# Between two halves of a gated attention and FFN kernel: one quarter's parts by way of HBM, a sum made from parts, copies and splits in another order

## The chip, the cores and the metric

One core of one Trainium2 chip. The metric is the device time of one execution in microseconds (us), the median of several runs. Five engines work side by side on their own instruction queues: TensorE (PE) for matmuls, VectorE (DVE), ScalarE (ACT), GpSimd (POOL) and SyncE (SP, which issues most of the DMAs). Each queue is worked off in order, so an instruction that waits holds up everything behind it on its engine.

## The reference

For x of 2048 tokens by 512 columns (all float32):

```python
x = A_x
g = sigmoid((x * gate_w).sum(-1, keepdims=True))
q, k, v = heads(x @ wqkv)                  # 32 heads of 16
a = attention(q, k, v) @ wo                # token s sees s, s-2, ..., s-14
b = (gelu(x @ w_gate) * (x @ w_up)) @ w_down   # 512 -> 1792 -> 512
out = g * a + (1 - g) * b
```

Attention has a window of 8 keys at a distance of 2, so even and odd tokens never meet. The kernel calls the two sets parity 0 and parity 1.

## The kernel before, in words

**Numbers in parts.** For each operand of a matmul the kernel keeps two float32r parts: `hi` is a copy by ScalarE (L770, recorded as L746), and `lo` is the raw value minus `hi`, by VectorE (L773). A product is three matmuls: hi hi, lo hi, hi lo. A weight in parts takes twice its raw size.

**Products by Strassen's scheme.** The large products are cut in quarters a11 to a22 (tokens) and b11 to b22 (weights) and take seven block products instead of eight: a11 b11, a12 b21, s1 t1, s2 t2, s3 t3, s4 b22 and a22 t4, where s1 to s4 and t1 to t4 are sums of quarters (t3 = b22 - b12, t2 = t3 + b11, t4 = b21 - t2). One block (`block`, L788) is 4 row tiles of 6 matmuls, 128 rows by 512 columns. Its result lies in four PSUM banks: `acc0` to `acc3`, or four of tag `p`.

**Stages.** `start` (L825) makes keys and queries of parity 0, and it is there that all sums of the weight quarters are made for the first time; it stores t1 and t2 to HBM (`TS`). Then comes `ffn(0)`, the FFN of the even tokens in 14 steps f, each with gate and up products (L430) and the down product (L473). Then `kq_second` (L1077), in this text **the turn**: keys and queries of parity 1 in seven blocks. Then `ffn(1)`, `out_first` and `finish` (L679), which multiply the attention's results by wo.

**Getting ready for the turn.** `before` (L545) and `ready` (L1040) are generators. During the last steps of `ffn(0)` they are advanced one step at a time, and their steps load raw weights (`load_raw`, L810, 512 KB each into a tile of tag `S`), load the stored t2 (`load_pairs`) and split operands. b11 is loaded raw in `before` and split in `ready`, b12, b21 and b22 are loaded at the head of `ready`, s1 is made at its end.

**The turn itself.** U are the four `acc` banks, V_ and Z_ four banks of tag `p`. a11 b11 goes into U. `out_of` (L798) copies U into V_, so that U can go on with s2 t2 and a12 b21 can be added in V_. Then `put` evicts V_ as keys and queries of tokens, U goes through s2 t2, s3 t3 and a22 t4 with copies `u2` and `u3` between them, and the last two blocks, s1 t1 and s4 b22, are joined with the copies on VectorE (`join`, L801).

**What sets the order.** Splits, copies and sums in the turn go through three `Row` objects, `act`, `row` and `mms` (L734 to 748): each ties an instruction to the one before it on its engine, so ScalarE, VectorE and TensorE keep the order of the program there. All else is placed by a scheduler, which leaves each engine one fixed queue.

**Attention** is a generator too. `pull(budget)` (L336) adds to a credit and advances it until the credit is spent; each `block` of the turn calls it four times with `ASK`. Its work is put far back in priority (`BEHIND`) and is tied to the latest matmul (`paced`), so it fills VectorE: scores (L210, L213), softmax, and the weighted sum of the values (`mix`: L258, L262, L264, L266, then a transpose, L271, and a store to HBM by SP, L273). The results return as `raw<-os` (L657) and are split by L87 and L88 for `finish`.

**Values.** `values(par, jj)` (L172) makes v of one tile of tokens with matmuls of 258 or 256 columns (L130); those of parity 1 belong to the head of `ffn(1)`.

Of the kernel before, what the change touches and what calls it, by code (L numbers as in the profile page):

```python
# [10 lines left out]
F32 = mybir.dt.float32  # L11
# [5 lines left out]
P = 128  # L17
# [9 lines left out]
WA = 576  # L27
# [4 lines left out]
NU = D // UC  # L32
WARM = 16
FILLERS = 2
ASK = 1.0
BEHIND = 150
PACE = (0.9, 1.0, 1.12)
LOAD = 4.0
# [10 lines left out]
def tile_gated_mix(ctx: ExitStack, tc: tile.TileContext, xt, wqkv, wff, wo, out):  # L49
# [11 lines left out]
    def tl(tag, dt=F32):  # L61
        return pool.tile([P, COLS.get(tag, 512)], dt, name=tag, bufs=BUFS[tag])
# [58 lines left out]
    g = pool.tile([P, 2, NP], F32, name="g")  # L121
    stages = iter(["hh", "hl"] * 99)

    def qkv_mm(ps, par, jj, cb, kcs, c0=0, cn=512):
        t = slice((jj % BT) * P, (jj % BT + 1) * P)
        for kc in kcs:
            xh, xl = X[par, jj // BT, kc]
            wh, wl = WC[cb, kc]
            for n, (a, w) in enumerate(((xh, wh), (xl, wh), (xh, wl))):
                LAST[:] = [nc.tensor.matmul(ps[:, :cn], a[:, t], w[:, c0:c0 + cn], start=(kc == 0 and n == 0),  # L130
                                            stop=(kc == KC - 1 and n == 2))]

    KQ = {}

# [37 lines left out]
    def values(par, jj):  # L172
        for hh in range(2):
            ps = bank(f"acc{(2 * jj + hh) % BT}")
            qkv_mm(ps, par, jj, 1, range(KC), (CU, 0)[hh], (WQ, CU)[hh])
            take(ps, par, jj, hh, tag=None if jj < 5 else "c")
        pull(2.7)
        if jj == NP - 1:
            done.add((par, 1))
# [282 lines left out]
    def down(par, gr, t, b):  # L462
        if b == t == gr == 0:
            ACC.update((t, bank(f"acc{t}")) for t in range(BT))
        pp = bank("p") if b else ACC[t]
        if b and gr:
            nc.scalar.activation(pp, RT[BT + t], AF.Copy)  # L467
        ts = slice(t * P, (t + 1) * P)
        for i in range(2):
            hh_, hl_ = Hs[2 * gr + i, b]  # L470
            d = WD[2 * gr + i]
            for n, (a, w) in enumerate(((hh_, d[:, :512]), (hh_, d[:, 512:1024]), (hl_, d[:, :512]))):
                ins = nc.tensor.matmul(pp, a[:, ts], w, start=(i == 0 and n == 0 and gr == 0),  # L473
                                       stop=(i == 1 and n == 2), skip_group_check=True)
                if gr and b == t == 0 and not par:
                    ordered(ins, LAST[-1])
                LAST[:] = [ins]
        jj = BT * b + t
        if gr == NG - 1 and par:
            nc.scalar.activation(pp, pp, AF.Copy, scale=gc[:, par, jj:jj + 1])  # L480
            ACC[jj] = pp
        elif gr == NG - 1:
            st = tl("scsscscs"[jj])[:, :512]
            nc.scalar.activation(st, pp, AF.Copy, scale=gc[:, par, jj:jj + 1])
            nc.gpsimd.dma_start(out_v[2 * jj], st)
        elif b:
# [58 lines left out]
    def before():  # L545

        room_x(1)
        for k in range(2):
            for i, (n, blk, kc) in enumerate((("a11", 0, 0), ("a12", 0, 2))):
                OP_[n, k], SRC[n, k] = X[1, blk, kc + k], XR[k][:, i * 512:(i + 1) * 512]  # L550
        load_raw("b11", slots("g1", 4), 0, 0)
        yield
        for step in ((), ("a11", 0), (), ("a12", 0)):
            if step:
                hi(*step)
                lo(*step)
            yield

    def ffn(par):
        XOP.update(((n, kc), X[par, blk, kc + k]) for n, blk, k in (("a11", 0, 0), ("a12", 0, 2), ("a22", 1, 2))  # L560
# [195 lines left out]
    def slots(tag, n, w=512):  # L756
        t = tl(tag, F32R)
        return [t[:, i * w:i * w + 512] for i in range(n)]
# [47 lines left out]
        queue.dma_start(rows(QS[par, 1], jj), two[:, 1])  # L806

    TS = {n: dram.tile([4, P, 512], F32, name=f"w{n}") for n in ("t1", "t2")}

    def load_raw(n, rooms_, hh, half):  # L810
        raw = RAWS[n] = tl("S")
# [13 lines left out]
    def start():  # L825
# [26 lines left out]
        load_w(b12, 1, 0)  # L852
        load_w(b22, 1, 1)

        g1a = slots("g1", 4)
# [79 lines left out]
        put(2, V_[2])  # L935
        put(3, V_[3])
        shift(0, nc.sync, 0, BT - 1)
        for k in range(2):
            store("t1", 2 * k, d_[k], 2)
        Z_ = [bank("p") for _ in range(BT)]  # L940
# [96 lines left out]
                XOP[n, kc] = X[0, blk, kc + k]  # L1037
        done.update(((0, 0), (0, 2)))

    def ready():  # L1040

        q = Q2["q"] = [[XR[k][:, i * 512:(i + 1) * 512] for i in range(4)] for k in range(2)]
        load_raw("b12", None, 1, 0)
        load_raw("b21", slots("g0", 3, WA) + slots("c", 1), 0, 1)
        load_raw("b22", None, 1, 1)

        def load_pairs(n):
            t = [tl("d", F32R) for _ in range(2)]
            for k in range(2):
                OP_[n, k] = t[k][:, :512], t[k][:, 512:1024]  # L1050
                load(n, 2 * k, t[k], 2)

        load_pairs("t2")
        yield
# [10 lines left out]
        for k in range(2):  # L1065
            X[1, 1, k] = tl("rt", F32R), tl("rt", F32R)
        name("a21", [X[1, 1, k] for k in range(2)], [q[k][2] for k in range(2)])
# [3 lines left out]
        yield  # L1071
        both(hi, "s1")
        both(lo, "s1")
        yield
        Q2["t1"] = load_pairs

    def kq_second():  # L1077
        for _ in Q2["turn"]:
            pass
        q, s12 = Q2["q"], Q2["s12"]  # L1080
        t4 = slots("g1", 4)
        U = [bank(f"acc{t}") for t in range(BT)]
        block(U, "a11", "b11", True, ask=ASK)
        V_ = [bank("p") for _ in range(BT)]
        for t in range(BT):
            out_of(V_[t], U[t])
        name("t4", pairs(t4), halves(RAWS["b21"]))
        name("b22", pairs(slots("g1", 4)), halves(RAWS["b22"]))
        Q2["t1"]("t1")
        block(V_, "a12", "b21", False, ask=ASK)  # L1090

        def put(jj, ps):
            take_first(1, ps, jj, lambda o, i: act.activation(o, i, AF.Copy))

        for k in range(2):
            sub(s12[k], s12[k], q[k][0])
        both(hi, "s2")
        both(lo, "s2")
        sub(RAWS["b12"], RAWS["b22"], RAWS["b12"])
        name("t3", pairs([x for tag in "sssc" for x in slots(tag, 1)]), halves(RAWS["b12"]))  # L1100
        for t in range(BT):
            put(t, V_[t])
        shift(1, nc.sync, 0, BT - 1)
        both(hi, "t3")
        both(lo, "t3")
        block(U, "s2", "t2", False, ask=ASK)
        sub(RAWS["b21"], RAWS["b21"], RAWS["b11"])
        sub(RAWS["b21"], RAWS["b21"], RAWS["b12"])
        for k in range(2):
            sub(q[k][0], q[k][0], q[k][2])  # L1110
        u2 = [tl("hl")[:, :512] for _ in range(BT)]
        u3 = [tl("hh")[:, :512] for _ in range(BT)]
        both(hi, "s3")
        both(lo, "s3")
        for t in range(BT):
            out_of(u2[t], U[t])
        block(U, "s3", "t3", False, ask=ASK)
        both(hi, "a22", "t4")
        both(lo, "a22", "t4")
        for t in range(BT):  # L1120
            out_of(u3[t], U[t])
        wide = tl("g0")
        for kc in range(KC):
            SRC["v", kc] = raw = (wide[:, kc * WA:] if kc < 3 else tl("c"))[:, :WQ + CU]
            nc.sync.dma_start(raw[:, :CU], wqkv[1, 2, :, kc * WQ:kc * WQ + CU])
            nc.sync.dma_start(raw[:, CU:CU + WQ], wqkv[0, 2, :, kc * WQ:(kc + 1) * WQ])
            t = tl("d", F32R)
            WC[1, kc] = OP_["v", kc] = t[:, :WQ + CU], t[:, VL:VL + WQ + CU]
        block(U, "a22", "t4", False, ask=ASK)
# [4 lines left out]
        both(hi, "a21", "b22")  # L1134
        both(lo, "a21", "b22")
        for k in range(2):
            sub(q[k][1], q[k][1], s12[k])
        both(hi, "s4")
        both(lo, "s4")
        fetch_d(0)  # L1140
        for f in range(2):
            fetch_sums(f)
        for kc in range(2):
            hi("v", kc)
            lo("v", kc)
# [71 lines left out]
```

## Time and profile before

| | us |
|---|---|
| median of 3 runs | 623.4 (622.85 to 623.93) |
| profiled execution, its own time | 622.54 |
| span of the profiled execution | 620.8 |
| PE busy | 600.1 (97%) |
| DVE busy | 532.3 (86%) |
| ACT busy | 390.4 (63%) |
| the turn on PE, first block to last | 287.2 to 344.6 |

The page cuts the span in 40 slices of 15.5 us and gives the busy share of each in tenths, and for PE also the clock that it was granted. Three short stretches stand out, all between 262 and 340 us, where PE stands and the clock falls for a while after it has stood. DVE is nearly as full as PE, ACT has room. DMA moved 132.6 MB.

In the lists, `p<-d,hh` means that a tile of the name p is written from tiles d and hh; `[3.50 <-ACT p L467]` says that the engine stood 3.50 us ahead of the instruction, and that an ACT instruction of line 467, writing p, let it go on. "x24" counts like instructions in a row, and their length is from the first's start to the last's end. Line L746 is the line of `Row`, which stands for every split, copy, sum and matmul that goes through it.

### The profile page before, as it was taken

The page shows a single profiled execution, that of the slowest core. Times are in us where ns is not written, and L with a number is a line of the kernel's source. Part 1 is how long each engine was busy: PE and PEld are TensorE (multiplying, and loading weights), DVE is VectorE, ACT ScalarE, POOL GpSimd, SP SyncE. Part 2 cuts the span into 40 slices and gives each one's busy share as a digit, 9 for nine tenths or more (in the row PEclk, how much of TensorE's full clock was granted, in tenths as well). Part 3 has the DMA queues.
Part 4 walks back from the last instruction along what each step waited for, and adds up shares of the span by engine and source line. Part 5 has one row for each costly group of instructions (what it writes and reads, how often), then busy time and mean ns, then how long its engine had stood idle before and what let it go on. Part 6 is the DMA issues. An engine that isn't in the chain of part 4 may idle for free.

```text
span 620.8 us, 8182 instructions
## 1 busy us (share of the span) xinstructions
PE 600.1 (97%) x2778; PEld 497.8 (80%) x2778; DVE 532.3 (86%) x618; ACT 390.4 (63%) x670; POOL 89.3 (14%) x121
## 2 busy tenths in 40 slices
PE   8999999999999999979697999999999999999997
PEld 6889977788887878858586998888888888888886
DVE  5997979999889898878979789999978898999821
ACT  5844557876887676856454345575757676784541
POOL 0501001111112121102003400110101110201300
PEclk9999999999999999989987999999999999999999
DMA  7689796988899898786616987787797786677723
GB/s 275 217 255 260 224 293 157 283 245 233 217 271 240 220 285 238 188 310 237 194 53 166 279 271 230 174 240 202 200 250 167 217 203 155 192 193 204 122 48 136
DMA packets 80305, 132.60 MB, mean 214 GB/s; under 512 B 8076, under 2 KB 46346, under 8 KB 80264
## 3 DMA queue, kind: packets, MB, share of 16 engines
q1 hardware_dynamic: 62588, 95.84, 47.8%
q0 software_dynamic: 12576, 32.97, 27.0%
q10 hardware_dynamic: 5100, 3.27, 1.7%
q8 instruction: 22, 0.36, 0.2%
q14 instruction: 19, 0.16, 0.1%
HBM read 67.77 MB, written 37.81 MB: 170 GB/s over the span
## 4 chain that ended last, share of the span: by engine, by line
PE 74%; DVE 9%; DMA 8%; issue 4%; ACT 3%; SPq 1%; ACTq 1%; POOL 0%; DVEq 0%; POOLq 0%
PE p L430 33%; PE p L473 11%; PE acc L473 10%; PE p L679 5%; PE acc L746 5%; PE p L746 4%; PE acc L130 4%; DVE prod L258 2%; PE acc L679 2%; DMA d<-r 2%; DVE prod L210 1%; DMA S<-wqkv 1%; DMA kq<-qs 1%; DMA prod<-wqkv 1%; DMA ws<-g 1%
## 5 line engine op out<-in xcount | busy, mean ns | idle before, releaser
L430 PE MATMUL p<-S,g 128*128 128x512 f32 x672 | 166.5, 390 | 0.0
L430 PEld LDWEIGHTS p<-S,g 128*128 128x128 f32 x672 | 125.4, 188 | 26.6 <-ACT rt L489 0.5
L430 PE MATMUL p<-A,g 128*128 128x512 f32 x504 | 127.5, 390 | 0.0
L430 PEld LDWEIGHTS p<-A,g 128*128 128x128 f32 x504 | 94.2, 188 | 19.9 <-DVE c L440 0.3
L210 DVE TENSOR_TENSOR prod<-kq 128x2048 f32<-128x2048 f32 x32 | 73.1, 2284 | 16.2 <-DMA kq<-qs 6.9
L388 POOL DMA_DIRECT2D g<-raw x40 | 34.6, 866 | 284.2 <-ACT g L387 201.8
L258 DVE TENSOR_TENSOR prod<-v,lg 128x2048 f32<-128x2048 f32 x32 | 72.8, 2275 | 3.0 <-PE acc L746 2.5
L213 DVE TENSOR_REDUCE lg<-prod 128x128 f32<-128x2048 f32 x32 | 73.0, 2281 | 0.3
L473 PE MATMUL p<-d,hh 128*128 128x512 f32 x224 | 69.2, 396 | 4.0 <-ACT p L467 3.5
L473 PE MATMUL acc<-d,hh 128*128 128x512 f32 x224 | 61.4, 391 | 1.5 <-DMA d<-r 1.0
L473 PEld LDWEIGHTS p<-d,hh 128*128 128x128 f32 x224 | 42.2, 190 | 14.7 <-ACT p L467 4.9
L473 PEld LDWEIGHTS acc<-d,hh 128*128 128x128 f32 x224 | 41.8, 188 | 11.7 <-DMA d<-r 1.8
L387 ACT ACTIVATE g<-raw 128x1024 fp32r<-128x1024 f32 (+1 forms) x40 | 39.4, 985 | 15.1 <-PE p L746 6.2
L392 ACT ACTIVATE g<-raw 128x1024 fp32r<-128x1024 f32 (+1 forms) x40 | 39.5, 990 | 12.4 <-PE p L430 12.4
L440 DVE TENSOR_TENSOR c<-p,s 128x512 f32<-128x512 f32 x56 | 37.9, 679 | 8.1 <-PE p L430 8.0
L130 PE MATMUL acc<-d,A 128*128 128x258 f32 (+1 forms) x288 | 40.9, 293 | 4.0 <-ACT d L746 2.9
L444 DVE TENSOR_TENSOR c<-c 128x512 f32<-128x512 f32 x56 | 38.2, 682 | 7.6 <-ACT c L541 7.3
L446 ACT ACTIVATE hh<-c 128x512 fp32r<-128x512 f32 x56 | 35.0, 625 | 14.9 <-DVE c L444 14.3
L473 PE MATMUL p<-d,hl 128*128 128x512 f32 x112 | 43.0, 396 | 0.0
L130 PEld LDWEIGHTS acc<-d,A 128*128 128x128 f32 x288 | 38.7, 201 | 5.4 <-ACT d L746 3.3
L435 ACT ACTIVATE s<-p 128x512 f32<-128x512 f32 x56 | 33.0, 592 | 15.8 <-PE p L430 13.9
L447 DVE TENSOR_TENSOR hl<-c,hh 128x512 fp32r<-128x512 f32 x56 | 38.2, 683 | 2.9 <-ACT hh L446 2.7
(181 smaller groups left out, 923.7 us busy)
## 6 DMA issues: line engine op xcount, KB each, us to landing
g<-raw POOLq DMA_DIRECT2D x27, 512.0 KB, 6.9
raw<-wff SPq DMA_DIRECT2D x42, 256.0 KB, 3.4
ws<-g SPq DMA_DIRECT2D x14, 768.0 KB, 5.9
g<-ws SPq DMA_DIRECT2D x14, 768.0 KB, 5.9
r<-wff SPq DMA_DIRECT2D x28, 256.0 KB, 3.9
d<-r POOLq DMA_DIRECT2D x24, 256.0 KB, 6.9
g<-raw POOLq DMA_DIRECT2D x13, 384.0 KB, 6.8
v<-vs SPq DMA_DIRECT2D x8, 512.0 KB, 6.0
```

The source lines that it names most:

```text
L130: LAST[:] = [nc.tensor.matmul(ps[:, :cn], a[:, t], w[:, c0:c0 + cn], start=(kc == 0 and n == 0), stop=(kc == KC - 1 and n == 2))]
L210: paced(nc.vector.tensor_tensor(prod, spans(k, jj), q[:, jj:jj + 2, None, :].to_broadcast([P, 2, W, UC]), op=OP.mult))
L213: nc.vector.tensor_reduce(two_of(lg, jj), prod.rearrange("p j w (h d) -> p (j w) h d", d=DH), axis=AX.X, op=OP.add)
L258: paced(nc.vector.tensor_tensor(prod.rearrange("p j w (h d) -> p (j w) h d", d=DH), spans(v, jj).rearrange("p j w (h d) -> p j w h d", d=D ...
L387: nc.scalar.activation(lo, raw, AF.Copy, scale=-1.0)
L392: ins = nc.scalar.activation(hi, raw, AF.Copy)
L430: LAST[:] = [nc.tensor.matmul(ps, w_, a_, start=(start and kc == 0 and n == 0), stop=(kc == 1 and n == 2), skip_group_check=True)]
L444: nc.vector.tensor_tensor(ge, ge, up, op=OP.mult)
L447: nc.vector.tensor_tensor(hl_, ge, hh_.bitcast(F32), op=OP.subtract)
L473: ins = nc.tensor.matmul(pp, a[:, ts], w, start=(i == 0 and n == 0 and gr == 0), stop=(i == 1 and n == 2), skip_group_check=True)
L679: ins = nc.tensor.matmul(pa, a, b, start=(first and n == 0), stop=(last and n == 2), skip_group_check=True)
L746: return lambda *args, **kw: self.add(getattr(self.eng, name)(*args, **kw))
```

## The change

- b11's two parts are no longer made a second time. `start` stores the tile with both (1 MB, one DMA by SP) in a new HBM tile `TB`, and `before` loads it back in one DMA in place of the raw b11; its splits on ScalarE and VectorE are gone.
- t4 is made as raw b21 minus the two parts of t2 (four subtractions of 128x512) in place of b21 minus b11 minus t3 (two of 128x1024).
- The raw loads of b12, b21 and b22 and the splits of a11 and a12 move ahead, from `ready` into `before`; the splits of s2, and the difference and splits of t3, move ahead from the turn to the end of `ready`. Since `act` keeps the program's order, they now stand ahead of the copies of the first block (U into V_). t3 uses the slots of b21's neighbours in tag g0 and c.
- From then on the copies of a finished block stand ahead of the splits of later ones; the splits of s3, a22, t4, b22, s4 and a21 each move about one block earlier, and the loads of the v weights too.
- The last products of ffn(0) are evicted to other tiles (rt in place of s and c for half of them), so X[1, 1] takes its tiles later.
- `values` of parity 1 for the first two tiles are ordered behind the last matmul that went through `mms`, that is behind s4 b22.
- `ASK`, the attention credit for each row tile of a block, goes from 1.0 to 0.7.

```diff
-ASK = 1.0
+ASK = 0.7
...
+                if behind:
+                    ordered(LAST[-1], behind)
...
-            qkv_mm(ps, par, jj, 1, range(KC), (CU, 0)[hh], (WQ, CU)[hh])
+            qkv_mm(ps, par, jj, 1, range(KC), (CU, 0)[hh], (WQ, CU)[hh], mms.last if par and jj < 2 else None)
...
-            st = tl("scsscscs"[jj])[:, :512]
+            st = tl("rt" if b else "sc"[t % 2])[:, :512]
...
     def before():
...
-        load_raw("b11", slots("g1", 4), 0, 0)
+        t = tl("g1", F32R)
+        nc.sync.dma_start(t.bitcast(F32), TB)
+        name("b11", pairs([t[:, i * 512:i * 512 + 512] for i in range(4)]))
         yield
-        for step in ((), ("a11", 0), (), ("a12", 0)):
-            if step:
-                hi(*step)
-                lo(*step)
-            yield
+        hi("a11", 0)
+        lo("a11", 0)
+        yield
+        load_raw("b12", None, 1, 0)
+        load_raw("b21", slots("g0", 3, WA) + slots("c", 1), 0, 1)
+        yield
+        hi("a12", 0)
+        lo("a12", 0)
+        yield
+        load_raw("b22", None, 1, 1)
+        yield
+        hi("a11", 1)
+        lo("a11", 1)
+        yield
...
+    TB = dram.tile([P, 2048], F32, name="wb11")
...
+        nc.sync.dma_start(TB, b11_.bitcast(F32))
...
     def ready():
...
-        for steps in (("a11", 1),), (("b11", 0),), (("b11", 1),), (("a12", 1), ("b21", 0)), (("b21", 1),):
-            for step in steps:
-                hi(*step)
-                lo(*step)
+        for step in ("a12", 1), ("b21", 0), ("b21", 1):
+            hi(*step)
+            lo(*step)
             yield
...
         both(hi, "s1")
         both(lo, "s1")
         yield
-        Q2["t1"] = load_pairs
+        for k in range(2):
+            sub(s12[k], s12[k], q[k][0])
+        both(hi, "s2")
+        both(lo, "s2")
+        yield
+        sub(RAWS["b12"], RAWS["b22"], RAWS["b12"])
+        both(hi, "t3")
+        both(lo, "t3")
+        yield
...
     def kq_second():
...
         block(U, "a11", "b11", True, ask=ASK)
         V_ = [bank("p") for _ in range(BT)]
         for t in range(BT):
             out_of(V_[t], U[t])
+        for k in range(2):
+            sub(q[k][0], q[k][0], q[k][2])
+        both(hi, "s3")
+        both(lo, "s3")
...
         block(V_, "a12", "b21", False, ask=ASK)
...
+        both(hi, "a22")
+        both(lo, "a22")
+        for k in range(2):
+            for part in OP_["t2", k]:
+                sub(SRC["t4", k], SRC["t4", k], part.bitcast(F32))
+        both(hi, "t4")
+        both(lo, "t4")
         for t in range(BT):
             put(t, V_[t])
...
         block(U, "s2", "t2", False, ask=ASK)
...
         for t in range(BT):
             out_of(u2[t], U[t])
...
+        both(hi, "b22")
+        both(lo, "b22")
+        block(U, "s3", "t3", False, ask=ASK)
+        for t in range(BT):
+            out_of(u3[t], U[t])
+        for k in range(2):
+            sub(q[k][1], q[k][1], s12[k])
+        both(hi, "s4")
+        both(lo, "s4")
+        both(hi, "a21")
+        both(lo, "a21")
...
         block(U, "a22", "t4", False, ask=ASK)
```

Lines of the changed kernel stand lower down: L746 becomes L759, L467 becomes L469, L130 stays.

More of the change, by code (lines that the diff above doesn't have):

```diff
@@ L122, in tile_gated_mix, with qkv_mm @@
     stages = iter(["hh", "hl"] * 99)
-    def qkv_mm(ps, par, jj, cb, kcs, c0=0, cn=512):
+    def qkv_mm(ps, par, jj, cb, kcs, c0=0, cn=512, behind=None):
         t = slice((jj % BT) * P, (jj % BT + 1) * P)
@@ L853, in start @@
         load_w(b22, 1, 1)
-        g1a = slots("g1", 4)
+        b11_ = tl("g1", F32R)
+        g1a = [b11_[:, i * 512:i * 512 + 512] for i in range(4)]
         t4_ = tl("g1", F32R)
@@ L1038, in start, with load_pairs @@
         done.update(((0, 0), (0, 2)))
+    def load_pairs(n):
+        t = [tl("d", F32R) for _ in range(2)]
+        for k in range(2):
+            OP_[n, k] = t[k][:, :512], t[k][:, 512:1024]
+            load(n, 2 * k, t[k], 2)
     def ready():
         q = Q2["q"] = [[XR[k][:, i * 512:(i + 1) * 512] for i in range(4)] for k in range(2)]
[L1043 to L1051, printed above, removed]
         load_pairs("t2")
+        name("t3", pairs(slots("g0", 3, WA) + slots("c", 1)), halves(RAWS["b12"]))
         yield
-        for steps in (("a11", 1),), (("b11", 0),), (("b11", 1),), (("a12", 1), ("b21", 0)), (("b21", 1),):
-            for step in steps:
-                hi(*step)
-                lo(*step)
+        for step in ("a12", 1), ("b21", 0), ("b21", 1):
+            hi(*step)
+            lo(*step)
             yield
@@ L1064, in ready @@
             name(n, [XOP[n, k] for k in range(2)], s12 if n in ("s1", "s2") else [q[k][n == "s4"] for k in range(2)])
-        for k in range(2):
-            X[1, 1, k] = tl("rt", F32R), tl("rt", F32R)
-        name("a21", [X[1, 1, k] for k in range(2)], [q[k][2] for k in range(2)])
         name("a22", [X[1, 1, 2 + k] for k in range(2)], [q[k][3] for k in range(2)])
@@ L1070, in ready @@
             row.tensor_tensor(s12[k], q[k][2], q[k][3], op=OP.add)
-        yield
         both(hi, "s1")
@@ L1081, in kq_second @@
         t4 = slots("g1", 4)
+        name("t4", pairs(t4), halves(RAWS["b21"]))
         U = [bank(f"acc{t}") for t in range(BT)]
+        for k in range(2):
+            X[1, 1, k] = tl("rt", F32R), tl("rt", F32R)
+        name("a21", [X[1, 1, k] for k in range(2)], [q[k][2] for k in range(2)])
         block(U, "a11", "b11", True, ask=ASK)
@@ L1086, in kq_second @@
             out_of(V_[t], U[t])
-        name("t4", pairs(t4), halves(RAWS["b21"]))
+        for k in range(2):
+            sub(q[k][0], q[k][0], q[k][2])
+        both(hi, "s3")
+        both(lo, "s3")
         name("b22", pairs(slots("g1", 4)), halves(RAWS["b22"]))
-        Q2["t1"]("t1")
+        load_pairs("t1")
         block(V_, "a12", "b21", False, ask=ASK)
@@ L1093, in put @@
             take_first(1, ps, jj, lambda o, i: act.activation(o, i, AF.Copy))
+        both(hi, "a22")
+        both(lo, "a22")
         for k in range(2):
[L1096 to L1100, printed above, removed]
+            for part in OP_["t2", k]:
+                sub(SRC["t4", k], SRC["t4", k], part.bitcast(F32))
+        both(hi, "t4")
+        both(lo, "t4")
         for t in range(BT):
@@ L1103, in kq_second @@
         shift(1, nc.sync, 0, BT - 1)
-        both(hi, "t3")
-        both(lo, "t3")
         block(U, "s2", "t2", False, ask=ASK)
[L1107 to L1110, printed above, removed]
         u2 = [tl("hl")[:, :512] for _ in range(BT)]
         u3 = [tl("hh")[:, :512] for _ in range(BT)]
-        both(hi, "s3")
-        both(lo, "s3")
         for t in range(BT):
             out_of(u2[t], U[t])
[L1117 to L1121, printed above, removed]
         wide = tl("g0")
@@ L1126, in kq_second @@
             nc.sync.dma_start(raw[:, CU:CU + WQ], wqkv[0, 2, :, kc * WQ:(kc + 1) * WQ])
+        both(hi, "b22")
[3 more added lines that the diff above has]
+            out_of(u3[t], U[t])
+        for k in range(2):
+            sub(q[k][1], q[k][1], s12[k])
[3 more added lines that the diff above has]
+        both(lo, "a21")
+        fetch_d(0)
+        for f in range(2):
+            fetch_sums(f)
+        for kc in range(KC):
             t = tl("d", F32R)
             WC[1, kc] = OP_["v", kc] = t[:, :WQ + CU], t[:, VL:VL + WQ + CU]
+            if kc < 2:
+                hi("v", kc)
+                lo("v", kc)
         block(U, "a22", "t4", False, ask=ASK)
@@ L1133, in kq_second @@
         done.add((1, 0))
[L1134 to L1145, printed above, removed]
         steps = chain(operands(1, 0, 0), operands(1, 0, 1))
```

## The prediction

> **What bounds the kernel now.** First the page's engine table, for the engine that is full:
>
> ```profile
> PE 600.1 (97%) x2778; PEld 497.8 (80%) x2778; DVE 532.3 (86%) x618; ACT 390.4 (63%) x670; POOL 89.3 (14%) x121
> ```
>
> TensorE is busy 600.1 of 620.8 us, and the change adds and takes away no matmul. So the time can only move by what PE loses, and the second view is the list of PE's waits over the turn (262 to 346 us), where the two halves of the kernel meet:
>
> ```profile
> PE acc L746 <- ACT hl L746: 5.8, 1, 5.8
> PE p L473 <- ACT p L467: 3.5, 1, 3.5
> PE acc L130 <- ACT d L746: 2.9, 1, 2.9
> PE acc L130 <- DVE d L746: 1.1, 1, 1.1
> ```
>
> Four stops, 13.3 us, at three places. The third view is PE's timeline there, which also shows the slow matmuls behind each stop (start, length, group, count, idle before it and its releaser):
>
> ```profile
> 273.62 0.94 PE L473 MATMUL p<-d,hh 128*128 128x512 f32 x2 [3.50 <-ACT p L467]
> ...
> 277.50 0.74 PE L473 MATMUL p<-d,hh 128*128 128x512 f32 x2
> ...
> 287.15 5.60 PE L746 MATMUL acc<-g,A 128*128 128x512 f32 x24
> ...
> 309.40 2.50 PE L746 MATMUL acc<-s,S 128*128 128x512 f32 x5 [5.76 <-ACT hl L746]
> ...
> 317.55 5.60 PE L746 MATMUL acc<-g,A 128*128 128x512 f32 x24
> 322.99 5.60 PE L746 MATMUL p<-d,S 128*128 128x512 f32 x24
> 331.49 1.68 PE L130 MATMUL acc<-d,A 128*128 128x258 f32 x8 [2.89 <-ACT d L746]
> 334.25 5.04 PE L130 MATMUL acc<-d,A 128*128 128x258 f32 x23 [1.08 <-DVE d L746]
> 339.12 5.62 PE L746 MATMUL p<-g,S 128*128 128x512 f32 x24
> 344.58 0.87 PE L130 MATMUL acc<-d,A 128*128 128x258 f32 x6
> ```
>
> At full rate a block of 24 takes 322.99 - 317.55 = 5.44 us, 0.227 a matmul. From these rows PE's loss:
> - Stop 1: 3.50 us, then 9 matmuls between 273.62 and 277.50 in 3.88 instead of 2.04: 1.84 more. Loss 5.3.
> - Stop 2: 5.76 us, then a block that takes 317.55 - 309.40 = 8.15 instead of 5.44: 2.71 more. Loss 8.5.
> - Stop 3: block s1 t1 ends at 322.99 + 5.44 = 328.43; until 339.12 only 31 small matmuls run (8 + 23). Six of those take 0.87 less about 0.16 of drain (5.60 against 5.44), 0.118 each, so 31 are 3.67 us of work in 10.69 us. Loss 7.0.
>
> Together 20.8 us in 76 us: the turn is bound by what feeds PE, by splits and copies in the queues of ScalarE and VectorE, while PE is the bound before and after it.
>
> **Stop 1, moved and kept.** The bank preload that released it stands behind a split of b11, which waits for its raw load:
>
> ```profile
> 270.43 1.15 ACT L746 ACTIVATE g<-S 128x512 fp32r<-128x512 f32 x2 [4.41 <-DMA S<-wqkv]
> ...
> 272.96 0.60 ACT L467 ACTIVATE p<-rt 128x512 f32<-128x512 f32 x1
> 262.66 2.38 SPq L812 DMA_DIRECT2D S<-wqkv  x4
> 260.00:262.00 2.00, 2.00 (x10) 1.67 (x9) 2.00 (x4) 1.97 (x3) 0.86 (x1) 1.00 1.00 184
> 270.00:272.00 2.00, 0.11 (x1) 0.00 (x0) 0.91 (x2) 1.57 (x4) 0.00 (x0) 1.00 1.03 414
> ```
>
> The first raw block, issued at 262.66, was there at 270.43, while the DMA engines moved up to 414 GB/s (last column of the two slices): bandwidth, not issue, sets it. b11's two splits on ACT (1.15 us) and two on DVE go. Its parts come from HBM as one load of 1 MB instead of 0.5 MB. By the instruction order of the changed kernel two more preloads now precede the next split on ACT, so PE runs 9 further matmuls, to about 272.1; but the one after stands behind the split of b21. In that order SP's 1 MB load waits for a matmul twelve places (2.7 us) ahead of the one that releases the first raw block, so it is issued near 260, then b12, then b21. b21 had been the third raw block: 270.43 plus two times 0.52 MB at 414 GB/s, 1.27 us each, 273.0. It is now second (271.7), with 1.05 MB ahead of it: 2.5 us, less what the slice from 260 to 262 has free, (414 - 184) x 2 us = 0.46 MB or 1.1 us: 273.1. I take 273.5, from 272 (all of the load hidden in the slack before) to 275 (none, and as much again for the four queues' turns). Then two splits and the preload: 273.5 + 1.15 + 0.60 = 275.2 us. Stop 1 becomes 275.2 - 272.1 = 3.1 us, and the slow stretch stays, 1.84. Behind it stand 42 matmuls, 9.5 us: a11 b11 starts at 275.2 + 9.5 + 1.84 + 0.13 (small gaps, as before) = 286.7 against 287.15, **0.45 us gained** (from -1.0 to +1.9).
>
> The slow stretch after a 3.1 us stop is the point where a rule speaks. In the rows above a 3.50 us stop was followed by 9 matmuls at nearly half rate, and stops of 2.89 and 1.08 us with eight matmuls between cost 7.02 - 3.97 = 3.05 us beside the stops themselves. The Trainium skill, "TensorE: Matmul & The Clock Gate", Part 1, says that the gate halves the clock only after an idle window of about 3.4 us, and that this window runs free of the kernel; by it a 3.1 us stop could leave the clock alone. The rows of the third place speak against a threshold between 2.89 and 3.50, so I keep the slow stretch; the other outcome is a rival.
>
> **A new stop 2.** In the old order the copies of the first block into the four p banks ran as its rows finished. In the new one ACT's queue, which is fixed in program order, has six splits ahead of them: of s1, s2 and t3. t3's waits for the difference b22 - b12, which is last in a chain on VectorE:
>
> ```profile
> 283.50 2.29 DVE L258 TENSOR_TENSOR prod<-v,lg 128x2048 f32<-128x2048 f32 x1 [0.23 <-PE acc L473]
> ...
> 296.66 1.21 DVE L746 TENSOR_TENSOR S<-S 128x1024 f32<-128x1024 f32 x1
> 298.77 1.15 ACT L746 ACTIVATE s<-S 128x512 fp32r<-128x512 f32 x2
> 307.57 1.29 ACT L746 ACTIVATE S<-raw 128x512 fp32r<-128x512 f32 x2 [7.64 <-DVE raw L746]
> 308.77 2.04 ACT L746 ACTIVATE hl<-acc 128x512 f32<-128x512 f32 x4
> ```
>
> The chain is the same 16 instructions in both kernels (two attention products of 2.29 us among them): from a matmul at 283.50 to about 297.8, 14.3 us. Before, it delayed only t3's own split (298.77), which nobody needed yet. Now it starts 0.45 earlier, ends at 297.35, t3's pair of splits ends at 298.5 (1.15), and the first copy at 299.1 (0.6; four take 2.04). a11 b11 ends at 286.7 + 5.44 = 292.1. So PE waits 7.0 us for a bank, and then runs slowly. I take 2.71 for that, as after the 5.76 us stop (the nearest length), with 1.84 as the other end. Cost: **9.7 us, new**. Behind the waiting split on ACT stand the copies and the splits of s3 and a22; the copies alone have PE waiting.
>
> **Old stops 2 and 3 go.** Stop 2 came from the copies of U behind s3's split, which waited 7.64 us for DVE. s3's difference is now made right behind that of t3, a block earlier (two of 128x512, some 1.4 us on DVE while PE does a12 b21), so the copies of U after s2 t2 find ACT free: 8.5 us back. Stop 3 came from values reading d parts just split; they now come behind the last block, s4 b22. Their splits stand between joins that end one block earlier; I put the room at 3 us by walking the order with these durations. Nothing new waits there: t4 is four differences of 128x512 in place of two of 128x1024 (at 0.69 and 1.21 us a piece, as the small and large products of DVE in the rows here, 2.8 against 2.4), beside a block of 5.44. Loss 7.0 back. b22's and s4's splits and the v loads come earlier, each a block or more ahead of its product: free, and up to 0.5 us if one delays a copy on ACT. The store of b11's parts at the start, 1 MB at 414 GB/s or 2.5 us of transfer, lies beside matmuls that don't wait for it; up to 1 us if it delays a load there.
>
> Sum, in the place of the 286.7: 286.7 + 5.44 + 9.7 + 6 x 5.44 = 334.4 us at the end of seven blocks. Before, they end at 344.56 with the 3.67 us of values already done: 340.9. **Gain 6.5 us.**
>
> **Attention, and the end.** ASK falls from 1.0 to 0.7 for 28 draws: 8.4 us of attention leaves the turn. In whole pieces these are two:
>
> ```profile
> 582.82 2.29 DVE L258 TENSOR_TENSOR prod<-v,lg 128x2048 f32<-128x2048 f32 x1
> 585.15 1.23 DVE L262 TENSOR_TENSOR prod<-prod 128x1024 f32<-128x1024 f32 x1
> 586.41 0.69 DVE L264 TENSOR_TENSOR prod<-prod 128x512 f32<-128x512 f32 x1
> 587.13 0.42 DVE L266 TENSOR_TENSOR o<-prod 128x256 f32<-128x256 f32 x1
> 587.59 0.71 DVE L271 STREAM_TRANSPOSE tb<-o 128x512 f32<-128x512 f32 x1
> 593.39 0.34 SPq L657 DMA_DIRECT2D raw<-os  x1
> raw<-os SPq DMA_DIRECT2D x1, 256.0 KB, 2.6
> 612.27 0.62 PE L679 MATMUL p<-S,hh 128*128 128x512 f32 x2
> 345.00:560.00 215.00, 215.00 (x1024) 180.87 (x1024) 196.25 (x206) 139.97 (x235) 26.21 (x32) 1.00 0.78 212
> ```
>
> A piece is 2.29 + 1.23 + 0.69 + 0.42 = 4.6 us; two, with part of a transpose, 9.5. I let all attention after the turn run 9.5 us later against PE. The last unit loses 3 us more, since its v load stands behind a multiply that moved: its last transpose ends at 600.8 in place of 588.3 on the old time scale. From there to a split tile is 8.8 us (588.3 to the load's issue at 593.39, 2.6 of landing, the load's row, a split of 0.6 and half a microsecond of ACT's other work): 609.6. PE wants it at 612.27. So **2.7 us of cover is left** of the 15 that there were; every us beyond it costs one.
>
> The profiled execution took 622.54 us around its span of 620.8; less 6.5 this is 616.0, and on the median of 623.4 us it is **616.9 us**.
>
> **Rivals.**
> - *The clock stays up after the first stop.* It is shorter than the 3.50 us one, and without the slow matmuls everything behind it comes 1.84 us earlier: 615.1. Against: the 2.89 us stop. The Trainium skill's page on the clock gate, named above, is for it.
> - *The first stop all but goes.* If b21 lands by 271, the stop is 0.6 us and the clock stays up: up to 3.1 + 1.84 = 4.9 us more, 612.0. For: bandwidth is the only thing behind it. Against: the DMA engines are full from 262 on, and the load is twice as large.
> - *The end is exposed in part.* The last attention runs 2 to 5 us past its cover: 618.9 to 621.9. For: the 2.7 us rest on chains of several steps. Against: VectorE has idle time to catch up.
> - *Attention becomes the bound, slower.* In the second FFN, VectorE is busy 196.25 of 215 us (fourth entry of the last row); its 18.75 us of gaps are waits on PE and ACT in a fixed order, in which a further piece pushes back the FFN's own products. If the whole 9.5 us lands on PE's path there or beyond the cover at the end, the time is 616.9 + 9.5 = 626.4. It decides from 6.5 us on. Against: the same row has PE busy for 215.00 of the 215 us.
> - *The change does nothing*: the new stop 2 is longer by the 6.5 us, say 13 to 14 us, because a third attention product stands ahead of the difference on VectorE: 622.2 to 624.6.
>
> **Numbers.** Runs of this kernel can tell 0.2% (1.2 us) from no change. The forecast (615.5 to 618.8, which takes in 272 to 275 for b21 and 1.84 or 2.71 for the slow stretch) has 0.48; the clock up 0.10; the first stop all but gone 0.08, and below 611.5 another 0.02; the end exposed 0.14; nothing 0.06; slower 0.12. Faster is 0.48 + 0.10 + 0.08 + 0.02 + 0.14 = 0.82. From 611.5 to 621.5 lie 0.48 + 0.10 + 0.08 + some 0.12: the range.
>
> **What would show it.** Right: a PE wait of about 7 us at the second block on ACT's copy into p, one of about 3 us near 272 on the bank preload behind b21's splits, no wait at the third to seventh blocks nor at values, and PE full to the end. Wrong: no wait at the second block, waits of PE behind 345 us, or PE waiting for the last hh near the end.

## The result, and the profile after

The changed kernel takes 614.58 us (median of 4 runs, 612.94 to 615.79) against 623.12 us before (4 runs, 622.18 to 623.93): the ratio is 0.9862, 95% interval 0.9833 to 0.9890, 8.5 us faster. In a second job it was 613.95 against 623.3 us, ratio 0.9858 (0.9827 to 0.9890). The forecast was 616.9, with a range from 611.5 to 621.5.

PE's line of the page and all its waits in the span (one at the very start left out):

```profile
PE 596.1 (97%) x2778; PEld 496.8 (81%) x2778; DVE 532.1 (87%) x618; ACT 393.1 (64%) x670; POOL 89.2 (15%) x121
```

```profile
PE p L759 <- ACT p L759: 6.8, 1, 6.8
PE p L475 <- ACT p L469: 3.3, 1, 3.3
...
PE acc L759 <- DVE A L759: 0.6, 1, 0.6
PE acc L475 <- DMA d<-r: 0.4, 1, 0.4
```

The matmuls are the same 2778. The 5.8 us stop at s3 t3 and the two ahead of the values (2.9 and 1.1) are gone, the first is about as long as it was (3.3 for 3.5), and one of 6.8 us is new. PE's timeline shows where:

```profile
264.53 2.88 PE L432 MATMUL p<-S,g 128*128 128x512 f32 x12
...
272.73 1.22 PE L475 MATMUL p<-d,hh 128*128 128x512 f32 x2 [3.28 <-ACT p L469]
...
284.95 5.60 PE L759 MATMUL acc<-g,A 128*128 128x512 f32 x24
297.40 2.50 PE L759 MATMUL p<-g,A 128*128 128x512 f32 x5 [6.84 <-ACT p L759]
...
305.16 5.60 PE L759 MATMUL acc<-d,S 128*128 128x512 f32 x24
...
326.92 5.60 PE L759 MATMUL p<-g,S 128*128 128x512 f32 x24
332.36 1.95 PE L130 MATMUL acc<-d,A 128*128 128x258 f32 x15
```

The stop of 3.28 us is again one for a bank preload (a copy by ScalarE into the PSUM bank that the matmul adds to), two preloads or nine matmuls further on. a12 b21 is the block that waits, 6.84 us, and takes 305.16 - 297.40 = 7.76 us in place of 5.44. From 305.16 to 332.36 five blocks take 27.20 us, 5.44 each: nothing is lost there any more. ScalarE and VectorE show what was waited for:

```profile
271.04 1.15 ACT L759 ACTIVATE g<-S 128x512 fp32r<-128x512 f32 x2 [4.91 <-DMA S<-wqkv]
...
295.71 1.15 ACT L759 ACTIVATE g<-S 128x512 fp32r<-128x512 f32 x2 [2.85 <-DVE S L759]
296.77 2.03 ACT L759 ACTIVATE p<-acc 128x512 f32<-128x512 f32 x4
```

```profile
281.30 2.29 DVE L260 TENSOR_TENSOR prod<-v,lg 128x2048 f32<-128x2048 f32 x1 [1.62 <-PE acc L475]
...
294.46 1.22 DVE L759 TENSOR_TENSOR S<-S 128x1024 f32<-128x1024 f32 x1
```

The four copies into p (296.77) come right behind t3's splits (295.71), which waited for VectorE's difference (from 294.46 to 295.68). That is 14.4 us behind the start of the chain at 281.30.

**A measure that leaves the run out.** Executions of one kernel differ by some us, and part of that lies before the turn. So the turn is measured inside a profile from the start of the last twelve gate and up matmuls ahead of it (264.53 above; this row of the profile before is below) to the end of the seventh block, less 0.118 us for each small matmul of values that lies in between.

```profile
267.23 2.88 PE L430 MATMUL p<-S,g 128*128 128x512 f32 x12
```

Before: 344.56 - 267.23 - 3.67 = 73.7 us. After: 332.36 - 264.53 = 67.8. At full rate it would be 63 matmuls and seven blocks, 14.28 + 38.08 = 52.4 us.

The medians below come from four jobs, in which the kernel before has 621.75 to 623.3 us; the turn and the stops come from one profile each.

| kernel | median us | the turn, us | PE's stops in it, us |
|---|---|---|---|
| before | 623.1 | 73.7 | 3.5, 5.8, 2.9, 1.1 |
| changed | 614.6 | 67.8 | 3.3, 6.8 |
| changed, again | 613.95 | 65.75 | 2.8, 6.8 |
| before_behind | 623.55 | 76.0 | 3.9, 5.8, 6.9 |
| no_behind | 615.2 | 68.0 | 4.5, 6.8 |
| copies_first | 614.7 | 68.3 | 4.3, 7.0 |
| copies_all | 616.4 | 69.1 | 3.7, 1.8, 5.8 |
| b21_ahead | 612.4 | 64.8 | 2.0, 6.8 |
| b11_raw | 614.1 | 66.8 | 3.0, 0.4, 6.8 |
| ask_one | 615.9 | 66.8 | 3.3, 6.8 |
| b21_late | 610.8 | 62.5 | 0.9, 6.8 |
| all_three | 611.8 | 65.1 | 2.0, 1.8, 5.8 |
| chain_ask | 606.9 | 59.5 | 5.1 |
| all_moves | 601.1 | 52.4 | none |

The first stop is 3.3 us in one profile of the changed kernel and 2.8 in the other, and 3.3 to 5.1 in the five runs that leave everything ahead of it as changed (no_behind, copies_first, copies_all, ask_one, chain_ask). So a gain of 1 us there is not read from one profile.

### The profile page after: what moved, and what is told of

Same layout as the page of the kernel before. It is cut to its first block, busy times and chain, and to the rows that moved or that the text cites. A ratio compares the mean times of both kernels' runs of the same rounds, so it can differ in the third digit from the quotient of the medians.

```text
span 612.0 us, 8200 instructions
## 1 busy us (share of the span) xinstructions
PE 596.1 (97%) x2778; PEld 496.8 (81%) x2778; DVE 532.1 (87%) x618; ACT 393.1 (64%) x670; POOL 89.2 (15%) x121
## 4 chain that ended last, share of the span: by engine, by line
PE 87%; issue 5%; DMA 4%; DVE 2%; ACT 1%; POOL 0%; SPq 0%; POOLq 0%; DVEq 0%; ACTq 0%
PE p L432 39%; PE acc L475 11%; PE p L475 10%; PE acc L130 7%; PE acc L759 6%; PE p L759 6%; PE p L692 5%; PE acc L692 2%; DMA d<-r 2%; DMA S<-wqkv 2%; DMA prod<-wqkv 1%; DVE S L759 1%; POOL g L390 0%; DVE r L759 0%; DVE prod L260 0%
## 5 line engine op out<-in xcount | busy, mean ns | idle before, releaser
L475 PEld LDWEIGHTS acc<-d,hh 128*128 128x128 f32 x224 | 42.1, 189 | 10.3 <-DMA d<-r 1.2
L264 DVE TENSOR_TENSOR prod<-prod 128x1024 f32<-128x1024 f32 x32 | 39.0, 1219 | 0.3
L130 PE MATMUL acc<-d,A 128*128 128x256 f32 (+1 forms) x288 | 37.9, 281 | 0.0
```

The source lines that it names most:

```text
L264: nc.vector.tensor_tensor(prod[:, :, :4], prod[:, :, :4], prod[:, :, 4:], op=OP.add)
```

## The experiments

### Old stop 3: the order of the values, or the parts of s4 and b22

before_behind gives the kernel before the change's one order, and no_behind takes it from the changed kernel:

```diff
-            qkv_mm(ps, par, jj, 1, range(KC), (CU, 0)[hh], (WQ, CU)[hh])
+            qkv_mm(ps, par, jj, 1, range(KC), (CU, 0)[hh], (WQ, CU)[hh], mms.last if par and jj < 2 else None)
```

> The kernel before with nothing changed but the order that holds the values of the first two tiles of parity 1 behind the last of the seven blocks. As the prediction has it (values are what stops there): old stop 3 loses its 3.97 us of standing and a part of the slow matmuls: 616 to 619.5 us. Rival (s4's and b22's parts and the joins are late by themselves, and the small matmuls only filled the gap): PE stands from the end of s1 t1 until VectorE's joins near 335 us, the 3.7 us of values come after it: 625 to 628 us.

> The changed kernel without the order that holds the values of the first two tiles behind the last of the seven blocks; the scheduler then puts 26 small matmuls between and inside s4 b22, as before. As the prediction has it (values reading parts just split make old stop 3, the order is what cures it): up to 3 to 4 us of stops come back, 617.5 to 618.5 us. Rival (the earlier splits of b22, s4 and the v weights cure it, the order is idle): the parts are ready about 5 us ahead of their reader in the changed kernel's profile, so 614.6 us within 1.

before_behind takes 623.55 us (10 runs) against 621.75 in the same job, ratio 1.0029 (1.0010 to 1.0048): slower, not faster, by 1.8 us where the rival had 2 to 5. Its PE waits:

```profile
PE p L748 <- DVE hh L748: 6.9, 1, 6.9
PE acc L748 <- ACT hl L748: 5.8, 1, 5.8
```

Without small matmuls to fill it, the old stop 3 is one wait of 6.9 us for a bank that VectorE's joins free. In the profile before, the joins stand on VectorE behind the lo parts of s4 and of the v weights; in the changed kernel they start while s1 t1 still runs (it ends at 326.92). The first three rows are from before, the last from the changed kernel:

```profile
332.30 1.28 DVE L746 TENSOR_TENSOR S<-raw,S 128x512 fp32r<-128x512 f32 x2
333.51 1.29 DVE L746 TENSOR_TENSOR d<-g,d 128x514 fp32r<-128x514 f32 x2
334.72 2.47 DVE L746 TENSOR_TENSOR hh<-p,hh 128x512 f32<-128x512 f32 x4
324.46 1.28 DVE L759 TENSOR_TENSOR hh<-p,hh 128x512 f32<-128x512 f32 x2
```

no_behind is at 615.24 us, its turn 68.0 as the changed kernel's. So the rival has the mechanism right in both: the values were not what stopped, and the order is idle. What is left is that the splits of b22 and s4, and with them the joins, come a block earlier in the changed kernel. That this gave the 7.0 us back is argued from these waits; it was not run by itself.

### The new stop 2: a place in ScalarE's queue, or VectorE's chain

copies_first puts s2 and t3 behind the first copies again; copies_all besides puts the splits of a22 and t4, with t4's sums, behind the copies of U:

```diff
         for t in range(BT):
             out_of(V_[t], U[t])
+        # from ready(): s2's difference and splits, t3's difference and splits
...
         for t in range(BT):
             out_of(u2[t], U[t])
+        # copies_all: a22's splits, t4's sums and splits
```

> The changed kernel with the splits of s2, t3's difference and its splits put back behind the copies of the first block into the p banks (program order, ScalarE and VectorE rows). Place in ScalarE's queue alone makes the new stop 2 (my theory): the stop of 6.84 us and the 2.3 us of slow matmuls behind it go, 9.2 us: about 605.4 us. VectorE's chain is the bound of the whole stretch (rival): the copies are no longer late, but the copies of U after s2 t2 still stand on ScalarE behind t4's splits, which end VectorE's chain near 307 us of the changed kernel's profile; PE stops ahead of s3 t3 for about 7 us instead and only some 2 us are gained: about 612.3 us.

> As copies_first, and besides the splits of a22, t4's four differences and its splits come behind the copies of U into u2 in program order, so that neither copy of a finished block stands behind a split that VectorE's chain feeds. If the stops follow the queue of ScalarE (copies behind waiting splits), both are gone now and only the real need of s3 t3 is left, whose parts VectorE finishes about 1 us behind the end of s2 t2: a stop of about 1 us, no slow matmuls, 8 us less than copies_first: about 606.8 us. If VectorE's chain bounds the stretch by its length, the stop of about 7 us moves once more, to a22 t4, whose parts come last in the chain: 613 to 615 us.

copies_first: 614.72 us. The copies of the first block come in time, a12 b21 waits for nothing, and the stop is back at s3 t3, with its slow matmuls; the row of PE, and what ScalarE does ahead of it:

```profile
309.47 2.50 PE L759 MATMUL acc<-g,S 128*128 128x512 f32 x5 [7.02 <-ACT hl L759]
```

```profile
304.77 0.63 ACT L759 ACTIVATE g<-S 128x512 fp32r<-128x512 f32 x1 [2.25 <-DVE S L759]
306.10 0.63 ACT L759 ACTIVATE g<-S 128x512 fp32r<-128x512 f32 x1 [0.70 <-DVE S L759]
...
308.75 2.14 ACT L759 ACTIVATE hl<-acc 128x512 f32<-128x512 f32 x4
```

The copies of U (308.75) stand behind t4's splits (304.77, 306.10), which wait for VectorE, and behind the 2 us of evictions of V_ that follow them. The rival's place is right; its 2 us of gain are not there. copies_all: 616.37 us, the stop moved once more, to a22 t4 (5.8 us, after one of 1.8 at s3 t3). Its VectorE:

```profile
301.91 1.35 DVE L759 TENSOR_TENSOR S<-raw,S 128x512 fp32r<-128x512 f32 x2
306.97 2.29 DVE L260 TENSOR_TENSOR prod<-v,lg 128x2048 f32<-128x2048 f32 x1 [3.71 <-DMA ks<-hl]
309.18 1.29 DVE L759 TENSOR_TENSOR A<-raw,A 128x512 fp32r<-128x512 f32 x2
310.38 0.69 DVE L759 TENSOR_TENSOR S<-S,d 128x512 f32<-128x512 f32 x1
```

VectorE stands 3.7 us behind s3's parts, since an attention product is queued ahead of a22's parts and t4's sums. The row puts the wait down to a DMA; the kernel ties each such product to the latest matmul (`paced`), and this one starts as PE ends the first row tile of s3 t3, at 306.9. So the tie is the likelier cause, but it was not tried by itself. Place alone doesn't cure the stop, in either form. chain_ask takes the copies and the evictions ahead of later splits on ScalarE, keeps t4's sums directly behind s3's parts on VectorE, and moves that attention product:

```diff
+        for t in range(BT):
+            put(t, V_[t])
+        both(hi, "s3")
+        both(lo, "s3")
+        # t4's four sums here; a22's and t4's splits behind the copies u2
...
-        block(U, "s3", "t3", False, ask=ASK)
+        block(U, "s3", "t3", False)
...
-        block(U, "a22", "t4", False, ask=ASK)
+        block(U, "a22", "t4", False, ask=2 * ASK)
```

> copies_first with both copies of finished blocks and the evictions of keys and queries ahead of later splits on ScalarE, t4's four sums directly behind s3's parts on VectorE, and the attention credit of block s3 t3 drawn in block a22 t4 instead, so that no attention product stands between t4's sums. Stop 1 as changed. If ScalarE's order and VectorE's chain together make the wandering stop of 7 us, and VectorE has the time when attention stands off for 10 us: no stop from the first block to the last beyond some 0.7 us at s4 b22, seven blocks in 39 us instead of 47.4: about 606 us. Rival: VectorE's work is too long for the seven blocks in any order (it was busy without a gap from 281 to 306 us), and the stop comes at the joins, s4 b22 or the values: 611 to 615 us.

606.91 us (604.06 to 610.2), ratio to before 0.9741 (0.9687 to 0.9796). The profile has no stop of PE inside the seven blocks: they run from 286.24 to 324.32, 38.08 us, 5.44 a block. That is the first theory, and VectorE's work does fit the seven blocks. Which of its three moves is needed was not tried one by one. From the turn's end to the end of the span it takes 281.5 us, the changed kernel 279.6, with a wait of PE of 1.1 us for VectorE at 384: some 2 us of the gain are lost there.

### Stop 1: b21's landing, its place, and b11

```diff
# b21_ahead, in before(): b21's raw load goes to SP's queue ahead of the load of TB
+        raw = RAWS["b21"] = tl("S")
+        first = nc.sync.dma_start(raw, wqkv[0, 1, :, :1024])
...
-        nc.sync.dma_start(t.bitcast(F32), TB)
+        ordered(nc.sync.dma_start(t.bitcast(F32), TB), first)
# b11_raw: the old load, and its splits in ready()
-        nc.sync.dma_start(t.bitcast(F32), TB)
+        load_raw("b11", slots("g1", 4), 0, 0)
# b21_late, in ready(): three empty steps, and an order behind the last bank preload
-        for step in ("a12", 1), ("b21", 0), ("b21", 1):
+        for step in ("a12", 1), (), (), (), ("b21", 0), ("b21", 1):
...
+                    ordered(act.last, PRE[-1])
```

> The changed kernel with b21's raw load issued ahead of the 1 MB load of b11's parts instead of two places behind it. Stop 1 is b21's landing behind 1.5 MB (my theory): b21 lands by 266 to 267 us instead of 271, its splits are done when PE comes to the bank preload, the stop of 3.28 us and the 2.70 us of slow matmuls go and all behind moves with them: about 608.6 us, stop 2 unchanged near 7 us. Rival: something else holds the preloads there (another landing, the x tiles, VectorE), and the stop shrinks by the 1.3 us of half a MB at most: 612.5 to 614.6 us. Second rival: the time won before the first block is lost at stop 2, because VectorE's chain starts from something that does not move: 614 us.

> The changed kernel with b11 loaded raw (512 KB) and split by ScalarE and VectorE as before, without the load of its parts; everything else as changed (t4 does not use b11's raw block). If the trip by HBM brought its two splits as a gain: 2 to 3 us slower, 616.5 to 617.5 us. If it only changed which split the bank preload waits for (b11's in place of b21's, each behind about 1.5 MB or less): stop 1 between 3 and 4 us as in the kernel before, 614 to 615.2 us.

> The changed kernel with b21's two splits held behind two more of the bank preloads on ScalarE; loads, sums and all else as changed. If stop 1 is the place of b21's splits in ScalarE's queue and nothing more: of its 3.3 us and the 2.7 us of slow matmuls some 1.3 us in two short stops are left (b21 lands near 271 us, the preload behind it comes at 272.7 where PE wants it at 272), 4.5 us gained: about 610 us. Rival: PE wants the next preloads' sources, gelu parts from VectorE, which are late by themselves, and a stop of 2 us or more with slow matmuls stays: 612 to 614.6 us.

b21_ahead: 612.43 us, a stop of 2.0 us where the first theory had none. b21 landed 7.7 us behind its issue at 261.58 (10.3 in the changed kernel) and was split from 269.35. That is 3.2 us behind the start of the last twelve gate and up matmuls; in the changed kernel it is 6.5 us (271.04 - 264.53). So the 1 MB ahead of it did hold it back. But in the order that the scheduler made of this edit the splits stand two preloads further ahead on ScalarE, and PE stops nine matmuls earlier, right behind the twelve. The time is near the second theory's, but its cause, something else than b21's load, is not what the rows show: landing and place act together. b11_raw: 614.11 us (611.76 to 616.54), as the changed kernel: the trip by HBM cost nothing and gained nothing that shows; in the changed kernel the preload only waits for b21 in place of b11. b21_late: 610.81 us, ratio 0.9812 (0.9782 to 0.9841), stop 0.9 us (1.3 expected): stop 1 was the place of a split in ScalarE's queue that nobody needed before 290 us.

### The draw of attention, and all of it together

```diff
-ASK = 0.7
+ASK = 1.0
```

> The changed kernel with ASK at 1.0 as before: more attention is drawn into the turn, less is left for the end. By the order of VectorE's queue the third piece of attention still comes behind t4's parts, so the stops stay as they are: 614.6 us within 1.5 (my theory: the draw is not what gained). Rival: the credit is what made room, and the 8.4 us of attention put back on VectorE delay the joins and the parts of s4 and the values: 617 to 620 us.

615.93 us (615.21 to 616.62), 1.3 us above the changed kernel. Against the kernel before in its own job the ratio is 0.9900, and 0.9862 for the changed kernel, which makes it 2.4 us: at the edge of the first theory, short of the rival. Its turn is not longer (66.8), so the draw is not what took the stops away. The time is lost behind the turn: from there to the end of the span it takes 281.6 us, and the nine profiles that draw as the changed kernel does take 279.5 to 279.6, a few values in the turn counted out. So some 2 us go with the larger draw, though only one profile of it exists; how they come about was not followed.

> copies_all with b21's raw load ahead of b11's parts, as in b21_ahead. If the two gains are in separate places they add: 2.2 us below copies_all, about 604.5 us. If VectorE's chain starts from something that b21's landing does not move, the second gain vanishes: as copies_all.

all_three (b21_ahead in copies_all): 611.76 us, 4.6 below copies_all where 2.2 were expected, the turn shorter by 4.0. The stops behind stop 1 keep their lengths (1.8 and 5.8), so what is gained at stop 1 carries over whole. The stop itself gives 1.7 of it (2.02 for 3.70 us); another 2.5 is luck of the clock, which stayed up here (rows in the next section).

> chain_ask and b21_late together, with b21's raw load ahead of b11's parts. If the places are separate the gains add: stop 1 gone whole (6 us) and the wandering stop gone (8.5 us), the end not exposed: 600 to 602 us. Rival: with the turn 14 us shorter the attention comes late at the end of the kernel, where 4.7 us of cover were left in the changed kernel's profile: 603 to 607 us.

all_moves (chain_ask, b21_late, and the load order of b21_ahead): **601.13 us** (599.64 to 601.34), ratio to before 0.9647 (0.9619 to 0.9675), the fastest here. PE's line and the clock's of its page, and its blocks:

```profile
PE 592.5 (99%) x2778; PEld 493.5 (82%) x2778; DVE 530.9 (89%) x618; ACT 391.7 (65%) x670; POOL 89.3 (15%) x121
...
PEclk9999999999999999999999999999999999999999
```

```profile
265.83 2.88 PE L432 MATMUL p<-S,g 128*128 128x512 f32 x12
...
280.11 5.60 PE L762 MATMUL acc<-g,A 128*128 128x512 f32 x24
...
312.75 5.60 PE L762 MATMUL p<-g,S 128*128 128x512 f32 x24
318.19 1.83 PE L130 MATMUL acc<-d,A 128*128 128x258 f32 x14
```

318.19 - 265.83 = 52.36 us: full rate, the turn has nothing left to give. Behind it the kernel takes 281.0 us where the changed kernel takes 279.6, with a wait of PE of 0.9 us for VectorE at 377. After that PE waits for nothing, so the end is not exposed.

> The changed kernel once more, on the same chip as these. If the 2.7 us by which the profiled execution reached the turn earlier than that of before belong to the change, PE starts its last group of twelve gate and up matmuls ahead of the turn at 264.5 us again within 0.5; if they are the run's, anywhere from 264.5 to 267.2 as in the other profiles.

It started the twelve matmuls at 265.36. In twelve profiles with the changed code ahead of the turn they start between 264.5 and 266.3, in the two with the old at 265.9 and 267.2. So most of the 2.7 us can be the run's.

## Why the prediction was right, and where it was not

- **Stop 1, moved and kept: right.** It put b21's landing at 273.5 us; ScalarE took it up at 271.04, 273.7 on the old scale (2.70 us, as the two rows of twelve matmuls differ). It put the stop at 3.1; it was 3.28, and 2.76 the second time. The slow matmuls behind it were mis-sized: 42 matmuls from 272.73 to 284.95 are 12.22 us for 9.52, so 2.70 in place of 1.84; 1.66 the second time. Stop and slow matmuls together cost 6.0 and 4.4 us where the forecast had 4.9 and the kernel before 5.3: 0.6 us lost and 0.9 gained, where the forecast had 0.45 gained. With 2.8 to 5.1 us for this stop in seven profiles, 3.28 so near to 3.1 is in part luck.
- **The clock.** The Trainium skill, "TensorE: Matmul & The Clock Gate", Part 1, has the clock halved only after an idle window of about 3.4 us. The runs do not show that threshold: in b21_ahead a stop of 2.02 us was followed by these slices (the clock is the figure behind POOL's):

```profile
271.04 0.73 PE L475 MATMUL p<-d,hh 128*128 128x512 f32 x2 [2.02 <-ACT p L469]
...
284.34 5.60 PE L761 MATMUL acc<-g,A 128*128 128x512 f32 x24
272.00:274.00 2.00, 2.00 (x8) 1.51 (x7) 1.97 (x4) 1.77 (x4) 0.00 (x0) 0.61 0.47 163
274.00:276.00 2.00, 2.00 (x7) 1.57 (x6) 0.87 (x2) 0.63 (x2) 0.00 (x0) 0.54 1.04 393
```

  51 matmuls take 13.30 us there for 11.56. Length alone doesn't decide it, though. In all_three the stop at the same place is as long, each slice from 270 to 284 us has 1.00, and the 51 matmuls take 11.69 us:

```profile
270.38 0.73 PE L475 MATMUL p<-d,hh 128*128 128x512 f32 x2 [2.02 <-ACT p L469]
...
282.07 5.60 PE L761 MATMUL acc<-g,A 128*128 128x512 f32 x24
```

  In the changed kernel the rival that kept the clock up did not occur, after 3.28 us or after 2.76, and keeping the slow stretch was right. What decides near 2 us stays open.
- **The new stop 2: right.** Forecast 7.0 us and 2.71 of slow matmuls; measured 6.84 and 7.76 - 5.44 = 2.32 (6.84 and 1.80 the second time). The chain of 14.3 us took 14.4. It starts from a matmul, so the 1 us by which stop 1 came out longer moved the chain and the first block alike. What the prediction didn't see is that this stop is not made by the place of t3's splits alone: with them out of the way it came back at the next block, and at the one behind that.
- **Old stops 2 and 3 go: right in size, wrong in cause for the third.** The five last blocks lose nothing any more, so all 15.5 us came back. The step "stop 3 came from values reading d parts just split" failed: before_behind shows s4 b22 waiting 6.9 us for late joins on VectorE, with the small matmuls as mere filling, and no_behind shows that the order of the values does nothing.
- **b11 by HBM, t4 from parts: nothing gained, nothing lost,** as costed; b11_raw shows it for b11. t4's four sums took 2.74 us (forecast 2.8); neither they nor the other tiles for the last products of ffn(0) were run by themselves.
- **The end: covered, as forecast.** The last transpose ended at 592.41, on the old scale of PE's end 601.1 for 600.8 forecast. The cover was 4.7 us, not 2.7 (the split ends at 598.85, PE wants it at 603.55):

```profile
591.70 0.71 DVE L273 STREAM_TRANSPOSE tb<-o 128x512 f32<-128x512 f32 x1
598.22 0.63 ACT L87 ACTIVATE hh<-raw 128x512 fp32r<-128x512 f32 x1 [8.34 <-DMA raw<-os]
603.55 0.62 PE L692 MATMUL p<-S,hh 128*128 128x512 f32 x2
```

- **The sum.** Forecast 6.5 us; the turn gave 5.8 in the first pair of profiles and 7.9 with the second of the changed kernel. The median moved by 8.5. In the first pair 2.7 us of the 8.8 between the spans lie before the turn, where the starts of the twelve profiles with the changed code are spread over 1.8 us. That part was in no step of the prediction; whether about 1 us of it is the change's stays open.
- **The slower rival** (attention as the bound) did not occur: PE has no stop from 333 us to the end in either profile of the changed kernel.

## What to carry to other kernels

A wait that is removed at its releaser may only move: after each move walk the queue of every engine in order and find the next instruction that stands in front of something late. Here one stop of 7 us wandered over three blocks until the copies stood ahead of waiting splits on ScalarE, the sums stood in a row on VectorE, and no filler was tied between them; the three moves together took the turn from 67.8 to 59.5 us, where copies alone had gained nothing. A split whose consumer is 20 us away has no business ahead of a bank preload: that cost 3.3 us and 2.7 more in slow matmuls (2.8 and 1.7 the second time). And what a stretch gains is not all gained by the kernel: with the turn at full rate, 1.4 us of it were lost again behind it.

## What the runs showed of the hardware

A stop of PE of 2.8 to 7.0 us cost a further 1.5 to 2.8 us in matmuls at a lower clock, and the cost does not grow with the stop: 1.66 after 2.76, 2.70 after 3.28, 1.87 after 7.02 (309.47 to the next block at 316.78), and 1.48 to 2.32 after the same 6.84 in seven profiles. Around 2 us it can go either way: a stop of 2.02 us cost 1.74 in one profile and 0.13 in another, at the same place. After stops of 1.77 us (5.73 for a block of 5.44) it was 0.3. Without any, PE in all_moves was granted the full clock in every slice, mean 1.000.
